# Attention's list planned anew, reciprocals spread by two transfers, four units of the next block moved into the list

## The chip, the cores and the metric

The program runs on one core of a Trainium2 chip, in one launch. The metric is the device time in microseconds. PE is TensorE, DVE VectorE, ACT ScalarE, POOL GpSimd and SP SyncE, which issues most DMAs. PEld is PE's loading of weights.

## The reference

Attention over 16 (batch, head) combinations, then two blocks of a two-matrix network on the 1152 x 512 result:

```
q_pool = mean of two neighbouring rows of q              # 1152 -> 576 rows, D = 64
scores = q_pool @ k.T / sqrt(64)                         # 576 x 1152 per head
attn   = exp(scores - max); attn /= sum(attn) + 1e-9
x      = attn @ v, heads side by side                    # 1152 x 512
h = x @ w_in;  P = a0 + a1 h + a2 h^2 + a3 h^3
g = P / (1 + |b0| |h| + |b1| h^2 + 1e-6);  x = g @ w_out     # first block, 512 -> 2048 -> 512
h = x @ w2_in; g = softplus(h);  out = g @ w2_out            # second block
```

There are 2 batches of 8 heads. The weights arrive as 64-bit numbers and are converted on the chip.

## The kernel before

Every precise product is made of three matmuls over split operands (high and low part): hi x hi, lo x hi, hi x lo. Heads are worked in pairs, `NP` = 8 of them; pairs 0 to 3 belong to the first batch. A pair takes nine steps t, one for each 128 of the 2 x 576 pooled query rows. A step makes three score tiles of 128 x 384 on PE (`score`), their maxima on DVE (`rmax`), exponentials with running sums on ACT (`expo`), transposes on PE with a split into two parts on ACT, DVE and POOL (`spread`). After steps 1, 4, 6 and 8 a group g of query rows is complete (`GT`, `GC`): `pv` multiplies it with v into a PSUM bank, high parts in rows 0 to 63 and low parts in rows 64 to 127.

The change is in what follows. `norm` (L881) sums the three denominators of a row on POOL and takes the reciprocal on DVE, one column per step in `RC`. `xev` (L896) transposes a broadcast of each reciprocal column on PE (`R`), so that 64 rows hold it; copies the lower half of the accumulator to `u` on ACT (`U`), adds the upper half on DVE (`U1`), and multiplies by the transposed reciprocals on DVE into `xs` (`U2`). `xout` (L924) rounds each half of `xs` to `xh` (`X0`) and takes the residue `xl` (`X1`), both on POOL. `xh` and `xl` are the input of the first block; `xs` has one buffer. Meanwhile the next pair is loaded, transposed and copied to its operand tiles through SP. `weight` prepares twelve weight tiles at the times `T["wt"]`, counted in steps (9 per pair): load on SP, two operations on ACT, three on DVE.

The order of all this is written out ahead. `op` (L512) records an operation with its engine, a duration, the keys that it reads and writes, and a time `when`: its step plus tuned offsets from the tables `O`, `OT`, `OJ`, `OF`, `OU`. `run` (L543) sorts each engine's operations by `when`, lets each engine take only the first of its queue (`beyond` looks further only if no head is free to go), assigns the 8 PSUM banks, and issues the operations in the order of the modelled starts. On the chip each engine then works in that order and waits where a result is late.

After attention's list the first block begins. A unit is one slice of 384 tokens (c) and one group of 128 hidden columns (f). A step k holds two units: `up` (12 matmuls each), three activations on ACT and three operations on DVE (`act1_a`, `act1_y`), logarithm and exponential on ACT (`act1_b`), three operations and a split (`act1_c`); two steps later come the down-projections (`down1`). The first eight units need only tokens 0 to 383, which pairs 0 to 3 make. In the block, `act` holds its activation tiles, in space freed after attention, and `wrb` holds late weight tiles, in the space of the even pairs' operands (`swap`).

Of the kernel before, what the change touches and what calls it, by code (L numbers as in the profile page):

```python
# [19 lines left out]
    xp=1,  # L20
# [17 lines left out]
    wt=(13.827, 23.117, 30.255, 39.714, 47.66, 61.48, 62.487, 63.019, 64.546, 64.568, 65.923, 67.055),  # L38
# [4 lines left out]
    whd=0,  # L43
    hh='A',
)
O = {
    "S0": -1.1791,
    "S1": -1.1966,
    "S2": -0.8221,
    "M0": -0.913,  # L50
    "M1": -0.9621,
    "M2": -0.7136,
    "B": -0.2834,
    "E0": -0.1512,
    "E1": -0.2925,
    "E2": -0.083,
    "T0": -0.1096,
    "T1": -0.0187,
    "T2": 0.3837,
    "V0": 0.3574,  # L60
    "V1": 0.47,
    "V2": 0.1866,
    "H0": 0.48,
    "H1": -0.0415,
    "H2": 0.7,
    "L0": 0.9316,
    "L1": 0.7,
    "L2": 0.852,
    "D0": 0.8392,
    "D1": 2.4795,  # L70
    "R": 2.5969,
    "U": 2.5174,
    "U1": 2.5202,
    "U2": 2.6796,
    "X0": 3.6534,
    "X1": 4.8093,
    "kq": -1.7841,
    "lv": 1.0305,
    "pq": 0.0502,
    "qt0": 0.6381,  # L80
    "qh0": 0.981,
    "ql0": 1.3317,
    "qt1": 1.9406,
    "qh1": 2.2316,
    "ql1": 2.4744,
    "dq0": 1.4222,
    "dq1": 1.9804,
    "dd": 3.7605,
    "kt0": 4.288,
    "kh0": 4.9547,  # L90
    "kl0": 5.0536,
    "kt1": 4.8793,
    "kh1": 5.9619,
    "kl1": 6.0298,
    "kt2": 4.8162,
    "kh2": 5.3835,
    "kl2": 5.7135,
    "dk0": 5.0813,
    "dk1": 7.9856,
    "v0": 5.2568,  # L100
    "v1": 3.7532,
    "w0": -0.8043,
    "w1": -0.3834,
    "w2": 0.0952,
    "w3": 0.6873,
    "w4": 0.9189,
    "wl": -4.3069,
    "W0": 0.36,
    "Y0": 0.36,
    "N0": 0.53,  # L110
    "W1": 0.358,
    "Y1": 0.47,
    "N1": 0.8012,
    "W2": 0.58,
    "Y2": 0.58,
    "N2": 0.75,
    "ft": 0.4933,
    "vw0": 7.4376,
    "vw1": 4.4384,
    "fh": -0.4564,  # L120
    "fp": 4.3153,
    "fl": 1.6433,
    "fa": -0.1275,
    "P0": 1.1239,
    "P1": 0.6123,
    "P2": 0.744,
    "P3": 1.4865,
    "P4": 1.2678,
    "P5": 2.3619,
    "P6": 1.4757,  # L130
    "P7": 1.785,
    "P8": 1.8288,
}
OT = {
# [35 lines left out]
}  # L170
OJ = {
# [1563 lines left out]
```

## Time and profile before

| quantity | value |
|---|---|
| median of 3 runs (lowest, highest) | 697.4 us (696.1, 698.19) |
| the profiled execution's own time | 696.2 us |
| its span | 694.3 us |
| granted TensorE clock | 1.00 throughout |
| PE busy | 671.7 us (97%), 4040 matmuls |
| DVE, ACT, POOL busy | 610.7, 502.9, 197.4 us |
| share of the DMA queue of SP in the time of 16 engines | 33.9% |

The page gives busy time per engine, a strip of 40 slices, the DMA queues, the chain that ended last and the costliest groups. Attention ends at about 288.6 us, the first block at about 494 and the second at the end. POOL works in attention only; in the rest PE, DVE and ACT share the work. A busy time is a union of the instructions' times, whose ends are modelled for matmuls; a row "before, releaser" is idle time of that engine in front of the group.

### The profile page before, as it was taken

The page shows a single profiled execution, that of the slowest core. Times are in us where ns is not written, and L with a number is a line of the kernel's source. Part 1 is how long each engine was busy: PE and PEld are TensorE (multiplying, and loading weights), DVE is VectorE, ACT ScalarE, POOL GpSimd, SP SyncE. Part 2 cuts the span into 40 slices and gives each one's busy share as a digit, 9 for nine tenths or more (in the row PEclk, how much of TensorE's full clock was granted, in tenths as well). Part 3 has the DMA queues.
Part 4 walks back from the last instruction along what each step waited for, and adds up shares of the span by engine and source line. Part 5 has one row for each costly group of instructions (what it writes and reads, how often), then busy time and mean ns, then how long its engine had stood idle before and what let it go on. Part 6 is the DMA issues. An engine that isn't in the chain of part 4 may idle for free.

```text
span 694.3 us, 11815 instructions
## 1 busy us (share of the span) xinstructions
PE 671.7 (97%) x4040; PEld 619.7 (89%) x4040; DVE 610.7 (88%) x1177; ACT 502.9 (72%) x1126; POOL 197.4 (28%) x357
## 2 busy tenths in 40 slices
PE   7999999999999988989999999999999999999997
PEld 5898989898889966978999999999999889889896
DVE  5899999999899999799999999999799999888722
ACT  4989999999999998777777778776566555455220
POOL 4778677676767753500000000000000000000000
PEclk9999999999999999999999999999999999999999
DMA  4582728374748433122203112210043223221012
GB/s 132 149 199 68 187 56 202 72 186 89 173 88 205 95 92 122 41 82 62 61 31 91 61 62 85 97 61 1 1 122 122 92 91 122 92 91 63 1 46 91
DMA packets 60396, 65.68 MB, mean 95 GB/s; under 512 B 21552, under 2 KB 49456, under 8 KB 60336
## 3 DMA queue, kind: packets, MB, share of 16 engines
q1 hardware_dynamic: 59152, 63.95, 33.9%
q10 hardware_dynamic: 1184, 0.98, 0.4%
q8 instruction: 32, 0.52, 0.3%
q14 instruction: 28, 0.23, 0.1%
HBM read 47.71 MB, written 2.36 MB: 72 GB/s over the span
## 4 chain that ended last, share of the span: by engine, by line
PE 38%; DVE 12%; ACT 4%; DMA 4%; issue 2%; POOL 1%; DVEq 0%; ACTq 0%; SPq 0%
PE acc L1478 14%; PE h L1409 7%; PE acc L1334 6%; PE h L1285 5%; PE h L1398 5%; DMA wraw<-in_moe_w_in_dram 3%; DVE m L1310 1%; DVE m L1320 1%; DVE p L1308 1%; DVE p L1319 1%; DVE p L1321 1%; DVE p L1309 1%; DVE pk L675 1%; DVE w L610 1%; DMA wraw<-in_moe_w_out_dram 1%
## 5 line engine op out<-in xcount | busy, mean ns | idle before, releaser
L797 ACT ACTIVATE p<-s,mb 128x384 f32<-128x384 f32 x216 | 124.6, 591 | 4.0 <-DVE mb L788 3.4
L784 DVE TENSOR_REDUCE nm<-s 128x1 f32<-128x384 f32 x216 | 111.9, 548 | 7.3 <-PE s L777 6.4
L748 PE MATMUL t<-ident,p 128*128 128x128 f32 x648 | 100.4, 275 | 5.0 <-ACT p L797 2.9
L1285 PE MATMUL h<-xh,w 128*128 128x384 f32 x384 | 98.0, 335 | 2.8 <-DVE p L1309 2.8
L1334 PE MATMUL acc<-gh,w 128*128 128x384 f32 x384 | 94.0, 337 | 1.6 <-ACT gh L1295 1.5
L748 PEld LDWEIGHTS t<-ident,p 128*128 128x128 f32 x648 | 77.9, 140 | 14.6 <-ACT p L797 10.4
L1478 PE MATMUL acc<-w,gh 128*128 128x512 f32 x288 | 89.7, 392 | 0.2 <-ACT gh L1421 0.2
L877 PE MATMUL pv<-ph,v 128*128 128x256 f32 (+1 forms) x288 | 89.7, 325 | 0.0
L610 DVE TENSOR_TENSOR pl<-t,ph 128x384 fp32r<-128x384 f32 (+1 forms) x160 | 79.0, 511 | 7.7 <-ACT ph L740 4.8
L877 PE MATMUL pv<-pl,v 128*64 128x256 f32 (+1 forms) x288 | 76.3, 295 | 0.1
L610 POOL TENSOR_TENSOR pl<-c,ph 128x384 fp32r<-128x384 f32 (+1 forms) x80 | 73.6, 928 | 3.2
L740 ACT CAST ph<-t 128x384 fp32r<-128x384 f32 (+1 forms) x160 | 69.2, 467 | 7.0 <-PE t L748 5.5
L1285 PEld LDWEIGHTS h<-xh,w 128*128 128x128 f32 x384 | 69.0, 188 | 3.9 <-issue 3.4
L1334 PEld LDWEIGHTS acc<-gh,w 128*128 128x128 f32 x384 | 68.6, 188 | 3.6 <-ACT gh L1295 3.6
L1285 PE MATMUL h<-xl,w 128*128 128x384 f32 x192 | 64.2, 334 | 0.0
L1478 PEld LDWEIGHTS acc<-w,gh 128*128 128x128 f32 x288 | 53.6, 188 | 10.6 <-ACT gh L1421 0.5
L610 DVE TENSOR_TENSOR gl<-p,gh 128x768 fp32r<-128x768 f32 (+1 forms) x60 | 47.5, 793 | 16.5 <-ACT gh L1421 14.8
L1334 PE MATMUL acc<-gl,w 128*128 128x384 f32 x192 | 60.0, 336 | 0.0
L877 PEld LDWEIGHTS pv<-ph,v 128*128 128x128 f32 x288 | 54.2, 188 | 2.6 <-ACT c L847 1.2
L1478 PE MATMUL acc<-w,gl 128*128 128x512 f32 x144 | 56.3, 393 | 0.0
L1409 PE MATMUL h<-xh,w 128*128 128x384 f32 x192 | 49.3, 336 | 0.0
L702 ACT CAST w<-pk 128x512 fp32r<-128x512 f32 x52 | 32.1, 622 | 21.2 <-DVE pk L675 21.1
(161 smaller groups left out, 1572.2 us busy)
## 6 DMA issues: line engine op xcount, KB each, us to landing
wraw<-in_moe_w_in_dram SPq DMA_DIRECT2D x32, 512.0 KB, 3.9
wraw<-in_moe_w_out_dram SPq DMA_DIRECT2D x32, 512.0 KB, 3.3
vr<-in_v_dram SPq DMA_DIRECT2D x8, 576.0 KB, 6.4
kr<-in_k_dram SPq DMA_DIRECT2D x15, 288.0 KB, 5.3
qr<-in_q_dram SPq DMA_DIRECT2D x15, 256.0 KB, 4.7
out_dram<-part SPq DMA_DIRECT2D x15, 128.0 KB, 1.8
qq1a<-qhi SPq DMA_DIRECT2D x8, 144.0 KB, 2.5
ks1a<-khi SPq DMA_DIRECT2D x4, 288.0 KB, 3.2
```

Source lines behind the costliest of these rows:

```text
L610: return eng.tensor_tensor(out=o, in0=a, in1=b, op=ALU.subtract)
L702: nc.scalar.copy(out=w[:, 0], in_=g)
L740: nc.scalar.copy(out=out, in_=in_)
L748: nc.tensor.transpose(o[0:rows, i * 128:i * 128 + n], a, ident[0:n, 0:n])
L784: op("M" + str(n % 3), "DVE", fn=lambda: nc.vector.tensor_reduce(out=NM[i][:, n:n + 1], in_=tl[k], axis=AX.X, op=ALU.max, negate=True), R= ...
L797: nc.scalar.activation(out=o, in_=tl[k], func=AF.Exp, bias=MB[i][:, t:t + 1], accum_out=DEN[i][:, n:n + 1])
L877: nc.tensor.matmul(out=o, lhsT=p, rhs=r[:, m, 0:w], start=(c == a == 0), stop=(c == C - 1 and a == 1))
L1285: nc.tensor.matmul(out=h, lhsT=w[:, wi, wd], rhs=x[:, d, xcols(c)], start=(n == 0), stop=(n == 3 * ND - 1))
L1334: nc.tensor.matmul(out=st["acc", c, d], lhsT=w[:, wi, wd], rhs=g, start=(first and n == 0), stop=(last and n == 2))
L1398: nc.tensor.matmul(out=o, lhsT=a[:, wi, d * 128:(d + 1) * 128], rhs=b[xi][:, d], start=(n == 0), stop=(n == len(mm) - 1))
L1409: nc.tensor.matmul(out=h, lhsT=w[:, wi, d * 128:(d + 1) * 128], rhs=x[:, d, xcols(c)], start=(n == 0), stop=(n == len(mm) - 1))
L1478: nc.tensor.matmul(out=st["acc", c, t], lhsT=g[:, t * 128:(t + 1) * 128], rhs=w[:, wi], start=(first and n == 0), stop=(last and n == 2))
```

## The change

1. `run` becomes a list scheduler. Each engine keeps the operations whose predecessors have all been planned, sorted by `when`. Among the first `AHEAD` = 10 (SP and the pseudo-engine X: the first alone), and within `WINDOW` = 6 steps of the earliest head, it takes the one with the least modelled start plus `RANK` = 50 ns per step of `when` behind the head. An operation that opens a bank needs one free bank, and one more for kinds other than `KEEP`. All offset tables and the twelve times `T["wt"]` have new values; the weights of the last pair go from 61.5 to 67.1 to 60.3 to 69.3.
2. `norm` works on three ranges of steps (0 to 4, 5 to 6, 7 to 8) instead of four. PE transposes the reciprocals once each range (2 or 5 columns to rows), DVE copies the rows to `RR`, SP writes them to a DRAM tile (`G0`) and reads them back spread over 64 partitions of `RB` (`G1`). `xev` only copies and adds, into one tile `XS`; `xout` multiplies a half of `XS` by `RB`, on POOL, and in the last pair on DVE.
3. Units 0 to 3 (first block, c = 0) are recorded in attention's list as `unit0`, at steps 69 to 70.5 plus offsets (4.27 and more for their matmuls), with activations of half width (one unit each). The loop of the first block leaves them out.
4. The activation tiles take the space of the even pairs' operands; `wrb` is allocated after attention.

```diff
+    RT = ((0, 5), (5, 7), (7, 9))
+    RQ = ((0, 0, SQ), (1, 0, 320), (1, 320, SQ))
+KEEP = ("S0", "S1", "S2", "P0")
 def norm(j, a):
+        t0, t1 = RT[a]
+        x, q0, q1 = RQ[a]
...
+        k, n = ring("bk"), t1 - t0
+        op("R", "PE", fn=lambda: transpose(k, [(r, 128)], n), R=[("RC", i, a)], W=[k], new=[("bk", NB)], **mm(109))
+        op("RW", "DVE", fn=lambda: nc.vector.tensor_copy(out=RR[0:n], in_=tl[k][0:n, 0:128]), R=[k], W=[("RR",)],
+           **dve(128))
+        op("G0", fn=lambda: nc.sync.dma_start(out=DR[i].rearrange("(t p) -> t p", p=128)[t0:t1], in_=RR[0:n]),
+           R=[("RR",)], W=[("DR", i, a)], **spq(lat=T["g0"]))
+        op("G1", fn=lambda: nc.sync.dma_start(
+            out=RB[64 * x:64 * x + 64, q0:q1], in_=DR[i][x * SQ + q0:x * SQ + q1].partition_broadcast(64)),
+           R=[("DR", i, b) for b in ((0, 0), (0, 1), (2, 2))[a]], W=[("RB", a)], **spq(lat=T["g1"]))
 def xev(j, g):
-        op("R", "PE", fn=lambda: transpose(
-            rt, [(RC[i][:, t:t + 1].to_broadcast([128, 64]), 128) for t in GT[g]], 64),
-           R=[("RC", i, t) for t in GT[g]] + [k], W=[rt], new=[("bk", NB)], **mm(109 * len(GT[g])))
...
-        op("U2", "DVE", fn=fn, R=[rt, u], W=[(*xs, g)], new=[("xs", 1)] if g == 0 else (), **dve(w))
+        o = XS[64 * x:64 * x + 64, c0:c0 + w]
+        W = [("XS", g, h) for h in ((0,), (0, 1), (0, 1), (1,))[g]]
+        op("U", "ACT", fn=lambda: nc.scalar.copy(out=o, in_=tl[k][64:128, 0:w]), R=[k], W=W, **act(w))
+        op("U1", "DVE", fn=lambda: nc.vector.tensor_add(out=o, in0=tl[k][0:64, 0:w], in1=o), R=[k], W=W, **dve(w))
 def xout(j, half):
+        last = j == NP - 1
+        op("U2", "DVE" if last else "POOL", fn=lambda: (nc.vector if last else nc.gpsimd).tensor_mul(
+            out=XS[:, cs], in0=XS[:, cs], in1=RB[:, cs]), R=[("RB", a) for a in range(2 + half)], W=X,
+           **(dve(HALF) if last else pool(HALF)))
 def run():
+                for when, i in queue[e][:1 if e in ("SP", "X") else AHEAD]:
+                    if e != "SP" and when > limit:
+                        break
+                    a = max(can[i], until[e])
+                    if i in opens:
+                        if len(f) <= (ops[i][4] in KEEP):
+                            continue
+                        a = max(a, min(f)[0])
+                    if ops[i][8]:
+                        a = max(a, lock[e])
+                    score = a + RANK * (when - queue[e][0][0])
+                    if best is None or score < best[0]:
+                        best = score, a, i
+    def unit0(u):
+        k, f = ring("bk"), u
...
+            op("mu", "PE", fn=fn, R=[w] + [(n, d, h) for n in ("xh", "xl") for h in range(2)], W=[k],
+               new=[("bk", NB)] if d == 0 else (), **mm(3 * 173))
...
+            op("ma", "ACT", fn=first(one(n, fn)) if new else one(n, fn),
+               R=[k, ("b",), ("a_",), ("wrb",) if new else ("acts", g)],
+               W=[("act", u, n)] + [("acts", g)] * new, **act(TOK))
...
+            op("my", "DVE", fn=one(n, fn), R=([k] if n == "p" else [("act", u, "s")]) + [("a_",)],
+               W=[("act", u, n[-1])], **dve(TOK))
 def attention():
-        at(te + T["cv"], lambda: op(0, "X", 0, swap(even, "wrb", NRB), W=[
+        at(te + T["cv"], lambda: op(0, "X", 0, swap(even, "ap", 2), W=[
...
+        for u in range(T["u0"]):
+            at(te + 6 + 0.5 * u, unit0, u)
 ... first block's loop
+                    if 2 * k >= T["u0"]:
+                        h = up(0, c, f)
+                if 2 * k < T["u0"]:
+                    ga[k] = [st["u", k][n] for n in "msp"]
```

## Rows read from the trace of the kernel before

**Rows 1.** The page's first lines: span, then busy time of each engine.

```profile
span 694.3 us, 11815 instructions
PE 671.7 (97%) x4040; PEld 619.7 (89%) x4040; DVE 610.7 (88%) x1177; ACT 502.9 (72%) x1126; POOL 197.4 (28%) x357
```

**Rows 2.** Busy time in stretches (start:end, length, engines with instructions, clock, DMA).

```profile
core 0: us, PE busy (x) PEld busy (x) DVE busy (x) ACT busy (x) POOL busy (x), PEclk, DMA share, GB/s
87.00:124.00 37.00, 36.63 (x261) 33.17 (x260) 33.88 (x84) 34.90 (x106) 27.80 (x50) 1.00 0.53 121
161.00:198.00 37.00, 35.64 (x249) 31.61 (x248) 33.86 (x85) 34.27 (x104) 24.80 (x45) 1.00 0.54 124
198.00:235.00 37.00, 36.98 (x269) 34.41 (x269) 33.18 (x86) 34.75 (x109) 28.04 (x52) 1.00 0.53 127
235.00:272.00 37.00, 30.61 (x200) 25.42 (x198) 36.16 (x81) 33.61 (x95) 17.82 (x33) 1.00 0.41 118
235.00:288.60 53.60, 46.70 (x320) 40.48 (x318) 48.76 (x113) 46.73 (x133) 28.02 (x53) 1.00 0.32 91
```

**Rows 3.** PE in order of time, two short stretches (start, us, instruction).

```profile
103.29 0.34 PE L777 MATMUL s<-ks0b,qq0b 128*128 128x384 f32 x1
103.46 0.33 PE L777 MATMUL s<-ks0b,ql0b 74*128 74x384 f32 x1
...
105.78 0.42 PE L777 MATMUL s<-ks0b,qq0b 128*128 128x384 f32 x1
106.04 0.33 PE L777 MATMUL s<-ks0b,ql0b 74*128 74x384 f32 x1
106.22 0.49 PE L748 MATMUL t<-ident,rc 128*64 128x128 f32 x3
106.46 0.39 PE L877 MATMUL pv<-ph,v 128*128 128x320 f32 x1
```

**Rows 4.** Groups from 0 to 300 us (busy, mean ns, idle before, releaser).

```profile
L784 DVE TENSOR_REDUCE nm<-s 128x1 f32<-128x384 f32 x216 | 111.9, 548 | 7.3 <-PE s L777 6.4
...
L919 DVE TENSOR_TENSOR xs<-t,u 64x256 f32<-64x256 f32 (+1 forms) x32 | 14.3, 448 | 2.8 <-PE t L748 0.7 <-issue 0.6
L748 PE MATMUL t<-ident,rc 128*64 128x128 f32 x80 | 14.2, 275 | 2.3 <-DVE rc L894 1.0 <-ACT c L847 0.8 <-ACT p L797 0.5
L610 POOL TENSOR_TENSOR xl<-xs,xh 128x288 fp32r<-128x288 f32 x16 | 13.2, 827 | 0.6
...
L788 DVE TENSOR_REDUCE mb<-nm 128x1 f32<-128x3 f32 x72 | 10.8, 150 | 0.6
...
L931 POOL CAST xh<-xs 128x288 fp32r<-128x288 f32 x16 | 7.0, 440 | 1.8 <-DVE xs L919 1.6
...
L888 POOL TENSOR_TENSOR rc<-den 128x2 f32<-128x2 f32 (+1 forms) x32 | 6.3, 197 | 39.1 <-ACT p L797 39.1
```

**Rows 5.** DMA issues (count, KB each, median us to landing).

```profile
qq0a<-qhi SPq DMA_DIRECT2D x6, 144.0 KB, 2.4
...
ks0b<-klo SPq DMA_DIRECT2D x3, 288.0 KB, 6.1
...
qdl<-qlo SPq DMA_DIRECT2D x12, 16.0 KB, 2.3
```

**Rows 6.** SP's queue in order of time, around its gap in one pair.

```profile
127.90 2.00 SPq L751 DMA_DIRECT2D qdl<-qlo  x2
136.49 0.46 SPq L751 DMA_DIRECT2D ks0a<-khi  x1
```

**Rows 7.** PE at the seam: last transposes, first and third step, first down-projection.

```profile
288.44 0.38 PE L748 MATMUL t<-ident,rc 128*64 128x128 f32 x2
288.57 0.60 PE L1285 MATMUL h<-xh,w 128*128 128x384 f32 x2
...
299.15 0.59 PE L1285 MATMUL h<-xh,w 128*128 128x384 f32 x2 [2.01 <-DVE p L1309]
...
308.73 1.69 PE L1334 MATMUL acc<-gh,w 128*128 128x384 f32 x8 [0.56 <-ACT gh L1295]
```

More of the change, by code (lines that the diff above doesn't have):

```diff
@@ L43 @@
     whd=0,
+    g0=2600,
+    g1=2600,
+    u0=4,
     hh='A',
@@ L74 @@
[L74 to L99, printed above, removed]
@@ new lines @@
+    "kl1": 6.6181,
+    "kt2": 5.3949,
+    "kh2": 5.2673,
+    "kl2": 6.8667,
+    "dk0": 1.8787,
+    "dk1": 9.933,
+    "v0": 7.923,
+    "v1": 4.6866,
+    "w0": -0.7162,
+    "w1": 1.9147,
+    "w2": 1.1261,
+    "w3": -0.0937,
+    "w4": -0.4796,
+    "wl": -2.1069,
+    "W0": 1.16,
+    "Y0": 1.16,
+    "N0": 1.33,
+    "W1": 0.2506,
+    "Y1": 1.27,
+    "N1": -0.4757,
+    "W2": 1.38,
+    "Y2": 1.38,
+    "N2": 1.55,
+    "ft": 2.6071,
+    "vw0": 10.3364,
+    "vw1": 5.6916,
+    "fh": -3.0412,
@@ new lines @@
+    "fp": 4.6307,
+    "fl": 1.7126,
+    "fa": -1.3028,
+    "P0": 1.5803,
+    "P1": 0.7811,
+    "P2": 0.0967,
+    "P3": 1.2433,
+    "P4": 2.8346,
+    "P5": 3.4166,
+    "P6": 1.4353,
+    "P7": 0.3875,
+    "P8": 0.0962,
+    "u0": 0.3577,
+    "u1": 0.489,
+    "a0": 0.8309,
+    "a1": 0.8472,
+    "a2": 1.2905,
+    "y0": 1.2098,
+    "y1": 2.4179,
+    "y2": 1.4617,
+    "b0": 2.3589,
+    "b1": 2.4468,
+    "c0": 2.7253,
+    "c1": 2.6455,
+    "c2": 3.1569,
+    "g0": 3.995,
+    "g1": 4.1361,
@@ L584, in beyond @@
-        def beyond(q):
-            for i in [i for i in q[1:] if i not in start][:40]:
-                x = ready(i)
-                if x:
-                    return x
-        with tc.manual_schedule():
-            while any(queue.values()):
-                heads = [x for x in (ready(q[0]) for q in queue.values() if q) if x]
-                a, i, bank = min(heads or [x for x in (beyond(q) for q in queue.values() if q) if x])
-                _, e, fn, _, _, _, ns, lat, port = ops[i]
-                queue[e].remove(i)
-                start[i], until[e] = a, a + ns
+                    preds[u[0]] += [(d, False) for d in tiles[m - n]]
@@ new lines, in run, with insert, choose @@
+        succ, todo, can = [[] for _ in ops], [len(p) for p in preds], [0] * len(ops)
+        for i, p in enumerate(preds):
+            for d, begun in p:
+                succ[d].append((i, begun))
+        queue = {e: [] for e in ENGS}
+        until, lock, owner = dict.fromkeys(ENGS, 0), dict.fromkeys(ENGS, 0), [None] * NB
+        def insert(i):
+            bisect.insort(queue[ops[i][1]], (ops[i][0], i))
+        def choose(limit):
+            f = [(0 if k is None else free[k], b) for b, k in enumerate(owner) if k is None or not left[k]]
+            pick = None
+            for e in ENGS:
+                best = None
+                for when, i in queue[e][:1 if e in ("SP", "X") else AHEAD]:
[11 more added lines that the diff above has]
+                        best = score, a, i
+                if best and (pick is None or best[1] < pick[0]):
+                    pick = best[1], best[2], min(f)[1] if best[2] in opens else None
+            return pick
@@ new lines, in run @@
+        for i in range(len(ops)):
+            if not todo[i]:
+                insert(i)
+        with tc.manual_schedule():
+            for _ in ops:
+                limit = min(q[0][0] for e, q in queue.items() if q and e != "SP") if any(
+                    q for e, q in queue.items() if e != "SP") else 1e18
+                a, i, bank = choose(limit + WINDOW) or choose(1e18)
+                when, e, fn, _, _, _, ns, lat, port = ops[i]
+                queue[e].remove((when, i))
+                until[e] = a + ns
```

778 lines of the change are left out of this document (403 added, 375 removed), and 225 rows, old and new, of tables (OT, OU).

## The prediction

> **What bounds the kernel now.** I read the page first [rows 1]: the span is 694.3 us, and PE is busy for 97% of it. That share is a mean over stages, so next come the stretches [rows 2]. Inside attention (87 to 124 and 198 to 235 us) PE is busy 36.63 and 36.98 of 37 us, ACT 34.90 and 34.75, DVE 33.88 and 33.18, POOL under 28.1: PE sets the pace and ACT stands 6% behind it. In the last pair of heads this turns over. From 235 to 272 us DVE is busy 36.16 of 37 us and PE only 30.61, because seven of the twelve weight preparations are laid there beside the attention work. From 235 us to the end of attention's list at 288.6, DVE has 4.84 us idle, ACT 6.87 and PE 6.90. Then comes the seam [rows 7]: the first block's up-projections start on PE at 288.57, the third step of them waits 2.01 us for VectorE and starts at 299.15, and the first down-projection starts at 308.73. The steps of the change therefore have different prices: PE work counts in the middle pairs, DVE work in the last one, and what is done before 288.57 shortens the seam.
>
> PE's 99% has to be weighed. Within the stretches PE's own weight loads (PEld) are busy 33.17 and 34.41 of 37 us, and the number of matmuls in 37 us goes from 249 (161 to 198 us) to 269 (198 to 235), though PE is over 96% busy in both [rows 2]. So the same busy share hides up to 8% of difference in pace. The Trainium skill (Perfetto Trace Analysis, section "Identifying the Most-Contended Engine") says that matmul busy time is a poor measure of how near TensorE is to its limit, since pipelined matmuls overlap, and that the busy share of the weight loads should be read instead; by that rule PE has some 10% left here, and removing PE work would give nothing by itself. The trace agrees that the share misleads. It speaks against my first term, and is rival 1.
>
> **The change, part by part.** All sums are against the profiled execution: 696.2 us, of which 694.3 are the span and 1.9 lie around it. It is 1.2 us under the median of the runs shown (697.4), and I add that at the end.
>
> *(a) Reciprocals through PE.* Before, a pair issues four groups of broadcast transposes, two of three and two of two. A group of three holds PE from 106.22 to 106.46, 0.24 us; a group of two from 288.44 to 288.57, 0.13 us [rows 3, 7]. After a transpose the next operation starts slower: a score's first matmul took 0.26 us to the next start (105.78 to 106.04) where one in a running sequence took 0.17 (103.29 to 103.46), so 0.09 us are added to each group [rows 3]. That is 2 x 0.33 + 2 x 0.22 = 1.10 us per pair. After, there are three single transposes; the third transpose of a group costs 0.24 - 0.13 = 0.11 us, so one is 0.20 with its restart and three are 0.60. PE saves 0.50 us per pair. I count it in the six middle pairs, where PE sets the pace: -3.0 us. Bounds: 0 if PE is not the limit, -4.0 if all eight pairs gain.
>
> *VectorE* loses four multiplications of 0.448 us per pair (1.8 us) [rows 4] and gets three copies of at most 5 x 128. No row shows such a copy; the nearest are 0.150 us for a reduction of three columns and 0.448 for the multiplication, and I take 0.2, nearer the smaller size: 0.6 us. The saving of 1.2 us a pair is priced at nothing in the middle pairs, since PE's work lies beside it; were VectorE the limit there, seven pairs would give 8.4 us. *POOL* gets two multiplications of 128 x 288 in seven pairs; the subtraction of that size and two inputs takes 0.827 us [rows 4], so 1.65 us per pair. POOL spent 39.1 us of attention waiting in front of the denominators' sums [rows 4], and is busy 75% [rows 2]: the cost is nothing. Without that cover it would be 11.6 us.
>
> *SP* gets six transfers per pair, and the second of each two waits on SP for the first to land. Behind it stand the loads of the next heads, the copies of keys and queries, and the weights; the next pair's transposes and scores wait for those. A landing takes 2.3 us for 16 KB, 2.4 for 144 KB and 6.1 us behind other traffic [rows 5]. SP has a gap from 129.90 to 136.49 us in one pair [rows 6], so I price it at nothing. If the cover goes, one blocked pair of transfers is 5 to 12 us late on SP, against a key copy issued some 15 us ahead of its use (136.49 against the next pair's scores around 152, an estimate from eight pairs of 34.8 us in the list that ends at 288.6).
>
> *(b) Four units ahead of the seam.* PE's third step of the first block can start where the list ends, without the two steps before it: 299.15 - 288.57 = 10.58 us go from the seam [rows 7]. They come back into the list. On PE they are the 48 matmuls of two steps, which take 10.58 - 2.01 (the wait) = 8.57 us there. On VectorE they are twelve half-width operations; the nearest row of 384 columns from the accumulator is 0.548 us [rows 4], so 6.6 us at most. The last pair's other edits there are -1.8 (multiplications) + 0.9 (two wider ones, which stay on VectorE in this pair) + 0.6 (copies) = -0.3. Thus +6.3 us go into 4.84 idle us from 235 us on: the list ends at least 1.5 us later even if every gap is filled, and at most 8.6 us later, if PE does the units in a row at the end. I take 4.1, nearer the lower end, because PE has 6.9 us idle in that stretch, the change spreads the weight preparations further to the end of the pair, and units have low priority and only fill. So (b) is -10.58 + 4.1 = -6.5 us (bounds -9.1 and -2.0). Late next is the first down-projection: ACT's logarithm and exponential and three VectorE operations stand before it, while PE does two steps, 8.6 us, that no longer wait.
>
> *(c) The list order.* The new planner takes, of the first ten waiting operations of an engine, the one that can start first by its cost model; the old one held to the tuned order. No row shows its result. The best and worst stretches bound it: at 269 instead of 261 matmuls per 37 us, the six middle pairs (209 us) take 6.2 us less; at 249, 10.1 us more [rows 2]. The mix of widths also moves these counts, so both ends are wide. I take -1, near to zero, since PE is already hardly idle there.
>
> Moving pools (activation tiles into the space of the even pair's operands, late weights into the space freed after attention) issues no instruction; at the seam it can only remove a wait on tiles still being read. Priced at nothing.
>
> **Sum:** -3.0 - 6.5 - 1.0 = -10.5; 696.2 - 10.5 = 685.7 us for one execution, 686.9 with the 1.2 us up to the median.
>
> **The rivals.**
> 1. *PE is not the limit.* ACT, which loses nothing, is at 94% [rows 2], and waits between engines may set the pace; then (a) and (c) give 0, and in (b) no idle time of VectorE is used: -10.58 + 6.3 = -4.3, so 693.1 us. For it: the uneven matmul counts. Against it: PE's idle time of 0.02 us in 198 to 235.
> 2. *Slower: the single output tile is freed late.* Multiplication, rounding and residue now wait for two chained transfers, all pairs share one output tile and one row tile, and ACT's copy into it stands in order before the next exponentials. Two landings of 2.3 to 6.1 us, and POOL's 0.197 x 3, 0.83, 0.44 and 0.83 us, make 7.3 to 14.9 us; five score steps, some 19 us, lie before the next copy into that half. Against it is that margin; for it, that POOL may leave the residue, a low-priority operation, until late, and that landings stretch behind weight loads. A stall of 1.5 us in each of seven pairs cancels the forecast; one of 2 us gives -10.5 + 14 = +3.5, so 700.9 us.
> 3. *The order does more.* All stretches run at the best pace and the gaps are filled: -3.0 - 6.2 - 9.1 = -18.3, so 679.1 us. For it: 6.9 us of PE idle before the seam. Against it: VectorE and ACT would have to be over 97% busy.
>
> **Chances.** Forecast 0.53, rival 1 0.20, rival 2 0.15, rival 3 0.12. Under 0.3% (2.1 us) a measurement of this kernel can't tell from no change. Faster by more: all of the forecast and rival 3, and three quarters of rival 1 (those below 695.3), 0.80. Same: a quarter of rival 1 and a little of rival 2, 0.07. Slower: 0.13. The range goes from below rival 3 (its third bound on (a), -1.0 more) to the worst order with the rest as forecast (-3.0 - 6.5 + 10.1 = +0.6, 698.0): 677 to 698.
>
> **What would show it.** Transposes from the reciprocals fall from 80 to 24 matmuls, the multiplication of the reciprocal leaves DVE except twice, and POOL has 14 of them near 0.83 us. The middle stretches hold more matmuls per 37 us with ACT nearer 37; if they hold 261 as before, (a) failed. The list ends near 290 to 293 minus what the middle pairs gave, and the first down-projection starts some 8 us after that, about 298 instead of 308.73. Rival 2 would show as ACT's copy of the accumulator waiting for POOL, or PE for a bank; a queue too slow as scores waiting for a transfer. The prediction is wrong if attention's list ends after 299 us, or if the seam still takes 20 us.

## The result, and the profile after

The changed kernel takes 703.6 us (median of 6 runs, 701.88 to 706.68) where the kernel before takes 697.8 beside it: ratio 1.0084, 95% interval 1.0058 to 1.011. It is 5.8 us slower. I had forecast 686.9 us and a range up to 698. The profiled execution took 703.66 us with a span of 701.4, against 694.3 in the profile of the kernel before, so 7.1 us of span are to be found; the profile before is one of that kernel's faster executions (696.2 us), which makes this 1.3 us more than the medians' difference.

The page's first lines of after, against [rows 1]: PE and VectorE have less work, 0.6 and 3.1 us, in a longer span.

```profile
span 701.4 us, 11747 instructions
PE 671.1 (96%) x3984; PEld 618.8 (88%) x3984; DVE 607.6 (87%) x1169; ACT 504.0 (72%) x1132; POOL 204.8 (29%) x347
```

The stretches of [rows 2], after (start:end, length, busy time and instructions of the engines, clock, DMA share, GB/s):

```profile
core 0: us, PE busy (x) PEld busy (x) DVE busy (x) ACT busy (x) POOL busy (x), PEclk, DMA share, GB/s
87.00:124.00 37.00, 36.55 (x263) 33.44 (x261) 33.40 (x85) 35.43 (x108) 29.16 (x49) 1.00 0.60 155
161.00:198.00 37.00, 36.37 (x263) 33.40 (x262) 33.97 (x84) 35.23 (x107) 28.21 (x47) 1.00 0.63 154
198.00:235.00 37.00, 36.33 (x254) 32.54 (x254) 33.09 (x84) 35.17 (x110) 30.04 (x52) 1.00 0.41 99
```

Two of the groups that answer to [rows 4], up to 300 us (busy, mean ns, idle before, releasers):

```profile
L1018 POOL TENSOR_TENSOR xs<-xs,rb 128x288 f32<-128x288 f32 x14 | 11.2, 803 | 10.3 <-DVE pk L766 3.5 <-DMA rb<-dr 1.9 <-DVE mb L880 1.6
L996 DVE COPY rr<-t 2x128 f32<-2x128 f32 (+1 forms) x24 | 6.6, 275 | 8.1 <-PE t L840 4.8 <-DMA dr<-rr 2.8 <-PE s L869 0.4
```

GpSimd's multiplications and VectorE's copies are there, with 0.80 and 0.28 us where I gave them 0.83 and 0.2; new is the 2.8 us of the copies' wait for a transfer.

The matmuls of the three stretches are 780 after and 779 before: the middle pairs run at the pace they had. The first score of the third and of the eighth pair says the same: 79.28 and 245.59 us after, 75.93 and 242.68 before, so five pairs take 166.3 us instead of 166.8. My step (a) asked for 2.5 us there.

What did change is the second pair. These are rows of after from SP, VectorE and PE in order of time (start, us, instruction, idle time before it and what ended it), then the stretches around them:

```profile
45.11 0.40 SPq L998 DMA_DIRECT2D dr<-rr  x1
48.47 0.47 SPq L1000 DMA_DIRECT2D rb<-dr  x1
...
48.54 0.28 DVE L996 COPY rr<-t 2x128 f32<-2x128 f32 x1 [2.49 <-DMA dr<-rr]
...
48.87 0.69 PE L869 MATMUL s<-ks1a,qq1a 128*128 128x384 f32 x1 [2.81 <-DVE rr L996]
...
45.00:50.00 5.00, 1.71 (x7) 1.22 (x7) 2.45 (x7) 2.25 (x7) 2.57 (x4) 0.76 0.54 158
50.00:55.00 5.00, 5.00 (x25) 4.87 (x25) 2.96 (x7) 2.89 (x8) 1.29 (x3) 0.55 0.42 101
```

Read them downwards: a transfer of 2.5 KB (5 x 128 numbers) out of the only row tile is issued at 45.11 behind the loads of the next pair and lands 3.4 us later. VectorE's next copy into that tile waits 2.49 us for it, in order, with its whole queue behind it, and PE waits 2.81 us for VectorE. PE's granted clock then falls from 1.00 (2.4 GHz) to 0.76 and 0.55, near the lower of its two levels (1.2 GHz), and stays low while PE is busy for all of 50 to 55 us. This pair takes 36.8 us (42.50 to 79.28) where it took 33.2.

At the seam [rows 7], PE of after:

```profile
298.09 0.28 PE L969 MATMUL pv<-ph,v 128*128 128x256 f32 x1
298.21 0.52 PE L1410 MATMUL h<-xh,w 128*128 128x384 f32 x2
...
308.83 1.01 PE L1474 MATMUL acc<-gh,w 128*128 128x384 f32 x2 [6.28 <-ACT gh L1420]
```

The list ends 9.6 us later than before, the seam on PE is 9.5 us shorter (10.6 instead of 20.2), and the first down-projection starts at the same time, 308.83 against 308.73. By this mark the change would cost nothing so far. But the mark hides work: before, four steps of up-projections (96 matmuls) are done ahead of it, after only three (72, of which 48 in the list). PE is 24 matmuls behind, some 4.2 us at 0.17 us each (an estimate from [rows 3]). It has waited 6.28 us for ACT's gated activations, while VectorE, which works ahead of these, had next to no gap from 300 to 310 us; the clock falls once more. The same stretches of before, and then of after:

```profile
305.00:310.00 5.00, 4.44 (x26) 4.12 (x25) 4.47 (x6) 2.40 (x4) 0.00 (x0) 1.00 0.02 6
310.00:315.00 5.00, 4.75 (x27) 4.16 (x25) 5.00 (x9) 3.95 (x6) 0.00 (x0) 1.00 0.15 31
```

```profile
305.00:310.00 5.00, 1.17 (x4) 1.18 (x5) 5.00 (x8) 1.60 (x3) 1.68 (x2) 0.71 0.11 25
310.00:315.00 5.00, 5.00 (x20) 4.97 (x19) 4.56 (x7) 4.77 (x7) 0.00 (x0) 0.61 0.53 186
```

**Where the 7.1 us are.** Behind 310 us the first block keeps both PE and VectorE all but full, so the account has to be kept in work done, not at marks of PE. Stretches of before and then of after (PE is the first busy time, VectorE the third):

```profile
0.00:240.00 240.00, 232.55 (x1635) 209.83 (x1636) 212.35 (x538) 215.85 (x649) 170.35 (x309) 1.00 0.57 136
240.00:310.00 70.00, 60.37 (x386) 53.47 (x385) 62.40 (x127) 57.04 (x140) 27.03 (x49) 1.00 0.29 90
310.00:480.00 170.00, 168.58 (x965) 166.55 (x964) 167.00 (x219) 129.11 (x174) 0.00 (x0) 1.00 0.20 63
```

```profile
0.00:240.00 240.00, 228.08 (x1571) 205.47 (x1572) 205.61 (x520) 213.52 (x641) 175.13 (x297) 0.99 0.55 139
240.00:310.00 70.00, 57.91 (x367) 50.39 (x366) 61.45 (x130) 56.60 (x148) 29.68 (x51) 0.98 0.29 86
310.00:480.00 170.00, 168.59 (x958) 167.35 (x956) 165.80 (x220) 128.15 (x175) 0.00 (x0) 0.99 0.24 74
```

PE is busy 168.6 of the 170 us behind 310 in both kernels, VectorE 167.0 and 165.8, so little of what is late at 310 can be made up. Of VectorE's 610.7 us of work before, 274.75 were done at 310, which leaves 336.0; of 607.6 after, 267.06 were done, which leaves 340.5. The change took 3.1 us of work from VectorE, and still 4.6 us more remain at the same point. The other 2.5 us of the 7.1 are idle time behind 310. Counted in the same way, PE has 378.8 us left before and 385.1 after, 6.3 more (its busy time also holds matmuls that the low clock has lengthened). So both engines are late at 310, and PE by more.

### The profile page after: what moved, and what is told of

It reads as the page before. It is cut to its first block, busy times and chain, and to the rows that moved or that the text cites. A ratio compares the mean times of both kernels' runs of the same rounds, so it can differ in the third digit from the quotient of the medians.

```text
span 701.4 us, 11747 instructions
## 1 busy us (share of the span) xinstructions
PE 671.1 (96%) x3984; PEld 618.8 (88%) x3984; DVE 607.6 (87%) x1169; ACT 504.0 (72%) x1132; POOL 204.8 (29%) x347
## 4 chain that ended last, share of the span: by engine, by line
PE 62%; ACT 16%; DVE 11%; DMA 6%; issue 3%; POOL 2%; SPq 1%; DVEq 0%; ACTq 0%; POOLq 0%
PE acc L1618 12%; PE acc L1474 11%; PE h L1410 10%; PE pv L969 6%; PE s L869 6%; ACT p L889 6%; PE t L840 6%; PE h L1538 5%; PE h L1549 4%; ACT ph L832 2%; DMA wraw<-in_moe_w_in_dram 2%; DMA dr<-rr 2%; ACT c L939 2%; DMA wraw<-in_moe_w_out_dram 1%; DVE nm L876 1%
## 5 line engine op out<-in xcount | busy, mean ns | idle before, releaser
L1474 PE MATMUL acc<-gh,w 128*128 128x384 f32 x384 | 97.0, 341 | 7.1 <-ACT gh L1420 7.1
L1410 PE MATMUL h<-xh,w 128*128 128x384 f32 x352 | 90.2, 334 | 1.3 <-DVE p L1439 1.3
L969 PE MATMUL pv<-ph,v 128*128 128x256 f32 (+1 forms) x288 | 87.8, 319 | 2.0 <-POOL ph L949 1.1
L1474 PEld LDWEIGHTS acc<-gh,w 128*128 128x128 f32 x384 | 70.3, 192 | 8.9 <-ACT gh L1420 8.5
L1410 PEld LDWEIGHTS h<-xh,w 128*128 128x128 f32 x352 | 63.5, 188 | 1.6 <-issue 1.6
L1618 PEld LDWEIGHTS acc<-w,gh 128*128 128x128 f32 x288 | 53.6, 188 | 10.6 <-ACT gh L1561 0.5
L1474 PE MATMUL acc<-gl,w 128*128 128x384 f32 x192 | 62.0, 340 | 0.0
L1410 PE MATMUL h<-xl,w 128*128 128x384 f32 x176 | 58.8, 334 | 0.0
L949 POOL CAST ph<-c 128x384 fp32r<-128x384 f32 (+1 forms) x80 | 37.7, 473 | 44.2 <-ACT c L939 33.0
L1549 PE MATMUL h<-xh,w 128*128 128x384 f32 x192 | 49.3, 336 | 0.0
```

What stands on the lines that cost most here:

```text
L949: nc.gpsimd.tensor_copy(out=view(h, o, w), in_=src(c, s0, w))
L969: nc.tensor.matmul(out=o, lhsT=p, rhs=r[:, m, 0:w], start=(c == a == 0), stop=(c == C - 1 and a == 1))
L1410: nc.tensor.matmul(out=h, lhsT=w[:, wi, wd], rhs=x[:, d, xcols(c)], start=(n == 0), stop=(n == 3 * ND - 1))
L1474: nc.tensor.matmul(out=st["acc", c, d], lhsT=w[:, wi, wd], rhs=g, start=(first and n == 0), stop=(last and n == 2))
L1549: nc.tensor.matmul(out=h, lhsT=w[:, wi, d * 128:(d + 1) * 128], rhs=x[:, d, xcols(c)], start=(n == 0), stop=(n == len(mm) - 1))
L1618: nc.tensor.matmul(out=st["acc", c, t], lhsT=g[:, t * 128:(t + 1) * 128], rhs=w[:, wi], start=(first and n == 0), stop=(last and n == 2))
```

## The experiments

All ratios are to the kernel before, run beside each. One question stands behind them: which of the change's parts costs, and what sets the pace of the list.

**The changed kernel with one thing altered.**

Three row tiles instead of one, the order unchanged:

```
-    RR = const.tile([5, 128], F32, name="rr")
+    RRS = [const.tile([5, 128], F32, name=f"rr{a}") for a in range(3)]
...
+        RR = RRS[a]
```

> The changed kernel (703.6 us) with three row tiles rr instead of one, one for each range of steps; the list order is the same. Theory A (the loss sits in two places: the one row tile that waits for its transfer in the first pairs, and the seam): the waits of 2.8 us before the copies to rr and PE's halved clock after them in 45 to 55 us go, pair 1 takes 33 us instead of 36.8: 3 to 4 us less, 700 us. Theory B (the new order is slower everywhere, the wait is a place where slack shows): under 1 us less.

Measured 699.8 us, 1.0026 (1.0013 to 1.004), so some 4 us of the 5.8 go with two more tiles of 5 x 128. The second pair, of this kernel:

```profile
45.00:50.00 5.00, 4.19 (x30) 3.58 (x30) 4.94 (x13) 4.70 (x14) 3.02 (x5) 1.00 0.57 164
50.00:55.00 5.00, 4.56 (x34) 4.24 (x32) 4.79 (x13) 4.28 (x13) 1.04 (x2) 1.00 0.39 103
```

The wait and the low clock are gone together, and this pair takes 33 us again (42.4 to 75.4). Shown: the single row tile cost about two thirds of the loss. How that divides between the wait and the clock behind it, no run separates.

No units in the list:

```
-    u0=4,
+    u0=0,
```

> The changed kernel without the four units in attention's list (u0 = 0); the first block does them after the list as before. Theory A (the units come back whole in the list, and the seam then waits 6.3 us with the clock down): the list ends near 290 us, the first down-projection starts near 310 with 96 instead of 72 up-projections behind it: 5 us less, about 698.5 us. Theory B: the last pair is as slow without them, 703 us or more. The step of my prediction that priced the units at -6.5 us would want 710 us.

Measured 707.9 us, 1.0134 (1.0108 to 1.016): inside this order the units gain some 3.5 us (by the ratios; 4.2 by the medians). The last product with the values starts at 296.87, only 1.2 us earlier than with them: they fit into gaps, as I had assumed. But the gaps are those of the new order: even without units this is 8.5 us later than before's 288.32. Part of it may be the clock, which is 0.90 in 240 to 310 us here and 0.98 with the units; so the gain isn't shown to be that of filled gaps alone.

The step after the units issued before the first down-projection, so that PE doesn't wait there:

```
+                if 2 * k == T["u0"]:
+                    for c, f in units[2 * k + 2:2 * k + 4]:
+                        w_need((0, 0, f))
+                        hs[k + 1] = up(0, c, f)
```

> The changed kernel with the second step after the seam (up-projections of units 6 and 7) issued before the first down-projection. Theory A (PE's order at the seam costs 6.3 us of idle time and the clock): PE fills 4.2 us of the gap, the clock stays at 2.4 GHz, 5 to 6 us less: 698 us. Rival (VectorE's chain to the first down-projection sets the seam and PE catches nothing up): only the clock's 2 us come back, 701.5 us.

Measured 702.9 us, 1.0071 (1.0052 to 1.009): about 1 us, less than the intervals can tell. PE's wait before the first down-projection falls from 6.28 to 2.15 us and PE has 3.3 us less left at 310, but VectorE has no less (342.0 us), and between 310 and 490 us PE now waits 6.0 us where it waited 1.8. Both alterations together:

> Both edits: three row tiles and the up-projections first. Theory A: the gains add, 694 us. Rival: 699 us.

Measured 698.6 us, 1.0007 (0.9994 to 1.0021): no difference from before that could be measured, and the best form of the change that I found. So these two places hold nearly the whole loss; why the change gains nothing beyond them is asked of its parts.

**Parts of the change alone, in the kernel before.**

The units in the old planner's list (with the early up-projection):

```
+        for u in range(T["u0"]):
+            at(te + 7.2 + 0.8 * u, unit0, u)
```

> The kernel before with the four units alone: recorded in its list (old planner, old tables, units placed from step 70 on), the second step after the seam issued before the first down-projection. Theory A (the units fill idle time of VectorE and PE at the end of attention, worth 4.3 us as between 707.9 and 703.6): 694 us. Rival (they only fill holes that the new order has made; the old order has 7.6 us of VectorE idle time there, and strict order can't use it): 698 us or more.

Measured 698.4 us, 1.0006 (0.9994 to 1.0018). In the old order the last product starts at 298.5 instead of 288.3: the units' 10 us come back in full, and nothing is gained. (This execution has a stretch of low clock, 0.67 in 270 to 275 us, that the profile before doesn't have.)

The new planner alone, with the old tables, old reciprocals and no units:

```
-                heads = [x for x in (ready(q[0]) for q in queue.values() if q) if x]
...
+                a, i, bank = choose(limit + WINDOW) or choose(1e18)
```

> The kernel before with the new planner alone (its own offset tables, old reciprocals, no units). Theory A (the list scheduler's order is what costs, since its modelled times are not the chip's): 702 to 708 us. Rival (the planner is neutral, the other edits cost): 697 to 699 us. The tables were tuned for the other planner, so a large loss alone doesn't convict it.

Measured 705.8 us, 1.0123 (1.0109 to 1.0138): 8.6 us slower by the ratio, the largest effect of a part but for the reciprocals below. Its stretches:

```profile
0.00:240.00 240.00, 230.51 (x1595) 206.16 (x1596) 211.49 (x529) 213.86 (x636) 169.74 (x304) 1.00 0.56 135
240.00:310.00 70.00, 60.44 (x375) 53.00 (x375) 56.94 (x124) 54.66 (x144) 28.55 (x54) 0.95 0.27 77
```

VectorE has been busy 268.4 us up to 310 where before it was 274.75, most of the difference from 240 on. But its total is 614.0 us here for the same 1177 instructions, so this busy time hides a part of the loss. PE's marks show it spread wider: from the first score of the second pair to that of the seventh pass 171.1 us (42.07 to 213.14) instead of 167.0 (42.68 to 209.70), and from there to the first up-projection behind the list 85.5 instead of 78.9. So some 4 us are lost in the second to sixth pair and 6.7 in the last two. (The old tables were tuned for the old planner, so this bounds the planner with its own tables from one side only.)

The reciprocals by transfers alone, in the old order, with three row tiles and places of my own:

```
+    "RW": 2.75,
+    "G0": 2.85,
+    "G1": 3.7,
+    "U2": 4.6,
+    "X0": 4.85,
+    "X1": 5.4,
```

> The kernel before with the reciprocals alone: single transposes, three row tiles, two transfers, multiplication on POOL; old planner. My step (a) (PE sets the pace of the middle pairs): 3 us less, 695 us. Rival (PE is not alone the limit; the middle pairs keep 33.2 us): 698 us, or a little more where VectorE waits for the transfers in the last pair.

Measured 744.8 us, 1.067 (1.0643 to 1.0697). The largest of its waits up to 300 us (engine, line, releaser: us in total, times, longest):

```profile
POOL xs L922 <- DMA rb<-dr: 45.2, 11, 5.8
```

GpSimd stands in order behind a transfer that lands later than planned, and the casts that everything waits for stand behind it. With the multiplication placed 0.8 of a step later ("U2": 5.4):

> The kernel before in its old written order, with the reciprocals by transfers, three row tiles, and GpSimd's multiplication placed 0.8 of a step (3 us) later than in the first try, behind the transfers' landing of up to 5.8 us late. Theory (no engine's work sets the pace; only waits count): if the waits of the multiplication for its transfer go, it is within 3 us of before, 695 to 701 us, since the 8 us of work taken from PE and VectorE was worth nothing in the cuts. The prediction's term would make it 3 us faster, 694 to 695. Rival: the in-order queues of GpSimd and SP pass each late transfer on whatever the place, 710 us or more.

Measured 735.0 us, 1.0551 (1.0537 to 1.0565). The wait shrinks to a third and others take its place:

```profile
POOL ph L852 <- ACT c L842: 34.2, 27, 7.2
DVE pl L604 <- ACT ph L735: 20.9, 31, 2.5
POOL rc L892 <- ACT p L792: 17.7, 13, 2.5
POOL xs L922 <- DMA rb<-dr: 16.5, 5, 4.6
```

So this part by itself could not be priced in the old order: 38 to 47 us is its price with my places, and whether others would do better was not found. As its rival had it, moving one operation moved the waits on to others.

**What sets the pace: work taken from one engine of the kernel before, its order kept.** From PE, the second matmul of 68 scores (4040 matmuls become 3972, where I had reckoned with 78 less; the output lacks their low parts):

```
-                                                   (QL[i][x][:, c0:c0 + 128], KS[i][x][0:74, ks]))]
+                                                   (QL[i][x][:, c0:c0 + 128], KS[i][x][0:74, ks]))[:1 if e == 0 else 2]]
```

> The kernel before, with one third of the 74-row score matmuls left out (66 of them, and 12 in the outer pairs' diagonal tiles, about 0.174 us each: 11 to 13 us of PE's work in attention), the list order unchanged; the scores are less exact. If PE sets the pace of attention: 9 to 12 us less. If the waits between engines or ACT set it: under 3 us less.

From ACT, the copies of the accumulator (VectorE then copies the other half where it added the two):

```
-            nc.scalar.copy(out=tl[u][:, 0:w], in_=tl[k][64:128, 0:w])
```

> The kernel before with ScalarE's copy of the accumulator's upper half left out (4 per pair, 32 in all; VectorE then copies the lower half where it added the two, so the low parts of the product with the values are missing in the output). ScalarE has 12 to 13 us less work in attention, in the same written order. Theory A, no single engine's work sets the pace of the middle pairs, only chains across engines that the written order fixed: 694 to 697 us, of which the most comes from 3.3 us that VectorE spent waiting for these copies. Theory B, ScalarE is the limit (94% busy in the middle pairs): 686 to 690 us.

From VectorE, the multiplications by the reciprocals (the addition writes their place, which gets a second buffer, and the output isn't divided):

```
-            nc.vector.tensor_mul(out=tl[xs][64 * x:64 * x + 64, c0:c0 + w], in0=tl[rt][0:64, o0:o0 + w],
-                                 in1=tl[u][:, 0:w])
...
```

> The kernel before with VectorE's multiplication by the reciprocals left out (4 per pair, 32 of 0.448 us, 14.3 us in all; the addition writes its place, and the output of attention isn't divided). Theory A, chains across engines in the written order set the pace: 694 to 697 us, as after the cut of PE's work. Theory C, VectorE's work is the limit, 92% busy in the middle pairs and 98% in the block behind: 685 to 690 us. The cut is also the part of VectorE's work that the changed kernel moved to GpSimd, so its time bounds what that move could give by itself.

Measured 697.65 us, 1.0001 (0.9987 to 1.0015); 695.75 us, 0.9978 (0.9963 to 0.9992); 696.9 us, 0.9987 (0.997 to 1.0004). By the durations of what is left out, each engine has 12 to 14 us less work; by the pages' busy times PE has 6.3 less, ACT 12.2 and VectorE 11.5. That gives nothing measurable on PE and VectorE and 1.5 us on ACT.

The profiled executions say a little more of PE. The five middle pairs take 164.4, 165.1 and 166.6 us in the three kernels instead of 166.8, so PE's cut did give 2.3 us there, of some 7 that it took (40 matmuls at 0.17 us). That execution ran at full clock and was the fastest of ten, 694.92 us; the median clock of the ten is 0.992, against 0.997 for the kernel before beside it. That a lower clock took the gain back is likely, and not separated.

So none of the three engines alone sets the pace of attention. That the waits between them do, in an order that was fitted to the durations it had, is the reading left, and is argued: no run cut two engines together. The VectorE cut shows such waits (its profiled execution, 700.8 us, was the slowest of its twelve, and its clock was 0.82 and 0.50 in 270 to 280 us):

```profile
0.00:240.00 240.00, 233.10 (x1633) 210.11 (x1634) 202.74 (x511) 215.44 (x648) 170.05 (x309) 1.00 0.56 135
240.00:310.00 70.00, 60.49 (x366) 54.03 (x365) 56.44 (x116) 55.63 (x139) 26.68 (x49) 0.93 0.29 91
```

With 11.5 us less to do it is busy 259.2 us up to 310, 15.6 less than before: it waits instead, and 4.1 us more lie behind 310.

**Attempts to mend the last pair**, on the 698.6 us kernel. In its trace two weight loads of 512 KB start together right behind four key copies, all four engines run short in 240 to 250 us, and the clock is 0.66 in the second half of that. First, these loads spread:

```
+        held = [("DR", 0, i - 5)] if i in (6, 7) else []
+        op("wl", fn=lambda: w_load(i), R=held, ...
```

> The changed kernel with three row tiles and the early up-projection (698.6 us), and two weight loads of 512 KB moved back on SP, each behind a transfer of reciprocals, so that they no longer start together right behind the last pair's four key copies. Theory: the burst of 2.1 MB there (DMA share 0.98, all four engines short of work in 240 to 250 us, clock 0.66 behind it) costs the last pair about 3 us: 695 to 697 us, clock 1.00 in 245 to 255 us, the last product with the values near 292 instead of 294.9. Rival: the last pair is long because of the planner's order itself; the loads' place is worth nothing: 698 to 699 us, or more where a preparation waits for its later load.

Measured 702.5 us, 1.0072 (1.0051 to 1.0092): my theory fell. The short stretch only moved to where the later weight is prepared, and is deeper there:

```profile
259.02 0.66 PE L869 MATMUL s<-ks1a,qq1a 128*128 128x384 f32 x1 [4.20 <-DVE w L701]
...
255.00:260.00 5.00, 0.98 (x3) 1.01 (x4) 3.77 (x9) 3.00 (x9) 1.17 (x2) 0.53 0.22 60
```

The units' VectorE reads placed behind ACT's, on top of that:

```
-            op("my", "DVE", fn=one(n, fn), R=([k] if n == "p" else [("act", u, "s")]) + [("a_",)],
+            op("my", "DVE", fn=one(n, fn), R=([k, ("act", u, "s")] if n == "p" else [("act", u, "s")]) + [("a_",)],
```

> As the kernel with the weight loads spread, and in the four units VectorE's reads of the accumulator come behind all three of ScalarE's, instead of between them. Theory: the 1.03 to 1.27 us waits of either engine for the other within a unit (some 5 us in the last 20 us of the list) go, and the list ends 1 to 2 us earlier: 694 to 696 us. Rival: VectorE sets the seam and is busy there anyway, so nothing is gained beside the kernel with the loads spread: within 0.7 us of it.

Measured 702.25 us, 1.0065 (1.0046 to 1.0084), as the rival said: ACT's two waits of 1.27 us for VectorE are gone and the time is not.

The planner told 7 us for a weight load:

```
-        op("wl", ..., **spq(lat=4000))
+        op("wl", ..., **spq(lat=7000))
```

> The kernel with the two weight loads spread (702.5 us), and the planner counts 7 us for a weight load instead of 4, so that it lays the preparation where the weight has landed. Theory: the 4.2 us wait of PE in 255 to 259 us and its clock of 0.53 come from a preparation that stands in order ahead of its weight: 696 to 698.5 us, no wait of PE over 2 us in 240 to 295. Rival: any other order of the last pair has its own waits of this size, since the planner's costs are off elsewhere too: 700 to 703 us.

Measured 709.7 us, 1.017 (1.0157 to 1.0183): slower still, against my theory. VectorE has done 259.2 us at 310 and has the most left of all:

```profile
0.00:240.00 240.00, 229.74 (x1596) 206.25 (x1597) 209.10 (x528) 217.03 (x652) 176.95 (x301) 1.00 0.57 142
240.00:310.00 70.00, 55.56 (x314) 47.90 (x312) 50.08 (x110) 49.38 (x130) 22.95 (x42) 0.88 0.23 71
```

The clock at the seam, held by doing one unit's 12 matmuls twice while PE would wait:

```
-                        hs[k + 1] = up(0, c, f)
+                        hs[k + 1] = up(0, c, f, 1 + (f % 2))
```

> The changed kernel with three row tiles and the early up-projection (698.6 us), and the 12 matmuls of the last unit of that up-projection issued twice (the first result is overwritten), 2.1 us more of PE's work where PE waits 2.16 us for the first gated activations. Theory A, VectorE sets the seam and the clock of 0.67 and 0.64 in 305 to 315 us only accompanies its wait: clock near 1.00 there, time 698 to 699.5 us. Theory B, the low clock costs the seam some 3 us of PE, and PE is late for the rest: 695 to 697 us.

Measured 701.2 us, 1.0054 (1.0034 to 1.0073), 2.6 us slower than without (3.3 by the ratios). The clock did hold, 1.00 from 305 to 315 us where it had been 0.67 and 0.64. But 17 us later PE waited 3.24 us for ACT's gated activations, with VectorE busy throughout, and lost the clock there:

```profile
305.00:310.00 5.00, 3.73 (x20) 3.11 (x19) 4.61 (x8) 4.45 (x7) 0.00 (x0) 1.00 0.42 131
...
320.00:325.00 5.00, 1.42 (x3) 0.92 (x4) 5.00 (x7) 2.24 (x4) 0.00 (x0) 0.72 0.00 0
...
322.84 1.01 PE L1472 MATMUL acc<-gh,w 128*128 128x384 f32 x2 [3.24 <-ACT gh L1418]
```

So full clock at the seam by itself brought nothing: PE came to wait for the same chain later. Why the held kernel is slower instead of even stays open.

**One account for all of them.** For each profiled execution, the work that VectorE and PE have left at 310 us (the total on the page less the busy time up to 310) against before's 336.0 and 378.8, and the span against before's 694.3:

| kernel | VectorE's work left | PE's work left | span |
|---|---|---|---|
| changed kernel | +4.6 | +6.3 | +7.1 |
| three row tiles | +1.6 | +2.5 | +3.0 |
| no units | +9.0 | +8.6 | +10.2 |
| early up-projection | +6.1 | +3.0 | +6.6 |
| both alterations | +1.3 | +1.0 | +1.5 |
| units alone | +1.3 | +1.7 | +0.5 |
| planner alone | +9.6 | +10.3 | +10.0 |
| PE's cut | -2.1 | -2.1 | -1.3 |
| ACT's cut | +1.1 | +0.9 | +0.8 |
| VectorE's cut | +4.1 | +4.4 | +4.6 |
| loads spread | +3.9 | +3.8 | +6.2 |
| and units reordered | +5.1 | +2.9 | +7.7 |
| clock held | +0.8 | -0.3 | +4.2 |
| load planned at 7 us | +12.8 | +11.0 | +13.4 |

For either engine the span is 310 us, its work left and its idle time behind 310, so each row is bookkeeping; what it can show is whose idle time stays the same. The larger of the two numbers is within 1.2 us of the span in eleven rows of fourteen, VectorE's alone in nine and PE's alone in eight. Where PE's work was moved ahead of 310 (early up-projection, clock held), PE waited more behind it and the span did not follow. So the block needs both engines on time; that is read from these rows, and no run cut work in the block itself. (The two kernels with the reciprocals alone don't belong here: their lists end long after 310.)

## Why the prediction was wrong

**Step (a), "PE sets the pace": the premise failed.** The transposes fell from 80 to 24 as forecast, and the pairs took as long as before; some 12 us of PE work less changed nothing (ratio 1.0001), with an interval of about 1 us to either side. The premise of my rival 1 held instead, though not its 693.1 us, which had no cost for the row tile and the order either. The rule of the Trainium skill that I had weighed (Perfetto Trace Analysis, "Identifying the Most-Contended Engine"), that matmul busy time is a poor measure of TensorE's room, agrees with these runs; I had read it and given its case 0.20. But the advice of that section of the Trainium skill, to optimize the engine with the highest occupancy first, would have brought little: relieved of 12.2 us, ACT at 94% gave 1.5, and VectorE at 92%, relieved of 11.5, gave nothing that could be measured.

**The edits priced at nothing: the row tile was not.** I looked at SP's queue and at the output tile and wrote of "one row tile" only in passing, in rival 2. The wait came in one pair of eight, at the place where a landing met the next pair's loads, and it was VectorE that stood in order behind it, not ACT and not GpSimd. One wait of 2.5 us became about 4 us; PE's clock fell behind it, and in 50 to 55 us PE at 0.55 was busy throughout while the others ran short. Rival 2 had the right kind of mechanism at the wrong tile. I had also read the 6.1 us of [rows 5] as a landing behind other traffic; it is that of loads of 288 KB, and the row doesn't say what was ahead of them.

On that landing the profile's waits of SP's queue say (after, up to 300 us):

```profile
SPq L1000 <- DMA dr<-rr: 65.1, 23, 4.5
```

That is 2.8 us for 1 to 2.5 KB on average, and 4.5 at worst. The Trainium skill (SBUF — State Buffer, "The DMA setup-cost knee") gives a roughly fixed 2 us per transfer, whatever its size; the mean here is above it, the worst, issued right behind a weight load of 512 KB, over twice that, and a short one, 1.1 us from its issue at 283.60, below it. The planner's tables count 2.6.

**Step (b), the units: right on PE's start times, mis-sized as time.** The seam on PE shrank by 9.5 us (I had 10.58) and the units themselves cost the list 1.2 (I had 4.1). But only some 3.5 us came of it in the new order and nothing in the old one. The first down-projection was to start at about 298 and started at 308.83, because ACT's gated activations were not ready. VectorE, which works ahead of them, is 97 to 98% busy from 310 us to the end of the block at 494, so the units help only as far as VectorE does their work in time that it would have waited. I had priced the seam by PE's start times though the row of the wait, 2.01 us for VectorE [rows 7], pointed at the other engine. My own alarm, a list that ends after 299 us or a seam of 20, did not go off: the list ended at 298.4 (295.7 with three row tiles) and the seam took 10.6. Both are start times, and neither counts the work that is done by then.

**Step (c), the list order: -1 forecast, +8.6 measured for the planner alone**, the largest miss of the sum. It lies inside the bound of +10.1 that I had worked out and then set aside as too far, but by luck: that bound was for the middle pairs, where the planner alone lost some 4 us, and the rest was lost in the last two, where weights are loaded and prepared. In the changed kernel, with the new tables, the middle pairs kept their pace and the last pair and the seam lost. What exactly makes the last pair longer was not settled: the burst of loads, the planner's 4 us for a load and the waits inside the units were each tried and each removal was worth nothing or less. Every new order of this list found its own waits of 2 to 4 us; that only the search over whole orders decides between them is argued from these runs, not shown.

The parts, in us: planner +8.6 (in the old kernel, with the old tables), row tile +4, units -3.5 (both in the changed one). They sum to 9 where 5.8 was measured. If parts measured in different kernels may be added, the rest, -3, is what the new tables and the reciprocals by transfers give together; these two were not separated.

## What to carry to other kernels

When the stage behind a seam keeps an engine or two all but full, price a change ahead of it by how much of each one's work is done at the seam, not by when one engine's first instruction starts. In a list where three engines are each over 90% busy and none alone is the limit, work taken from one may be worth next to nothing (here 0 to 1.5 us of 12), and a new order has to be priced by the waits that it makes. A single small buffer that is refilled only after a transfer out of it has landed is a wait on the engine that fills it, so count its tiles before its bytes.

## What the runs showed of the hardware

The granted clock of TensorE fell after single waits of PE: to 0.76 and 0.55 behind 2.81 us in the second pair, to 0.71 and 0.61 behind 6.28 us at the seam. It did not fall behind the 2.01 us of [rows 7]. But behind 2.00 us at the same step of the same block it did, in the kernel with the planner alone, where it was 0.50 from 310 to 313 us (a matmul of 384 columns takes 0.53 us there instead of 0.33):

```profile
309.25 0.58 PE L1300 MATMUL h<-xh,w 128*128 128x384 f32 x2 [2.00 <-DVE p L1324]
...
310.47 0.53 PE L1300 MATMUL h<-xl,w 128*128 128x384 f32 x1
```

Inside the list, too, nearly the same stretch could go either way: in the kernel before, in the kernel with the units alone (whose list is the same up to there), and with ACT's cut:

```profile
270.00:275.00 5.00, 3.36 (x23) 3.00 (x24) 4.45 (x13) 3.80 (x12) 0.35 (x1) 1.00 0.35 111
```

```profile
270.00:275.00 5.00, 3.59 (x15) 3.12 (x16) 4.22 (x13) 2.75 (x10) 0.00 (x0) 0.67 0.32 107
```

```profile
270.00:275.00 5.00, 4.03 (x18) 3.52 (x17) 3.64 (x11) 2.77 (x8) 0.05 (x1) 0.54 0.32 105
```

PE is busy 3.4 to 4.0 us in each, with 23 matmuls at full clock and 15 and 18 at the lower. The first two kernels arrive there with the same four waits of PE, 0.86, 0.36, 0.73 and 0.97 us; behind the last one the clock fell in the second of them alone:

```profile
272.23 0.41 PE L748 MATMUL t<-ident,rc 128*64 128x128 f32 x2 [0.97 <-DVE rc L894]
```

```profile
272.00 0.63 PE L752 MATMUL t<-ident,rc 128*64 128x128 f32 x2 [0.97 <-DVE rc L898]
```

So the waits alone don't tell whether the clock falls, and no run here shows what does. Executions of one kernel differ in time and in clock together: of the twelve with the units alone, the five at 0.995 took 696.65 to 696.95 us and the seven at 0.987 to 0.992 took 698.11 to 699.65. With VectorE's cut they differ by up to 5.8 us (695.04 to 700.79).

In the units ACT's second read of the accumulator waits for VectorE's read of it, 1.27 us in two of four. The Trainium skill (PSUM — Partial Sum Buffer, "PSUM bank collisions raise a hardware error") says that two engines must not touch one bank in the same quadrant of 32 partitions at the same time, two reads included. The order that the trace shows agrees with this, and the planner's costs don't have it.
